# A delta-rule recurrence with a gated MLP: two batches in lockstep on four TensorE quadrants, every engine in a fixed order

## The chip, the core and the metric

The kernel runs on one core of one Trainium2 chip. The metric is the device time of one execution in microseconds (us). The core's engines are TensorE (PE; its weight loads are shown apart as PEld), VectorE (DVE), ScalarE (ACT), GpSimd (POOL) and SyncE (SP), which issues nearly all transfers. Each engine works through its own instructions in order; between engines there are semaphores.

## The reference

Four batches, eight heads, 768 positions, head size 48. Each head carries a 48x48 state through all positions; the heads' outputs, side by side (384), go through a gated MLP with a mix over positions.

```python
def _attn_ref(q, k, v, beta):
    k_n = k / (np.linalg.norm(k, axis=-1, keepdims=True) + 1e-06)
    for t in range(S):
        kt, vt, bt = (k_n[:, :, t], v[:, :, t], beta[:, :, t, None])
        y[:, :, t] = np.einsum('bhd,bhde->bhe', q[:, :, t], state)
        v_old = np.einsum('bhde,bhd->bhe', state, kt)
        state = state + bt[:, :, :, None] * np.einsum('bhd,bhe->bhde', kt, vt - v_old)

def _moe_ref(x, w_in, w_spatial, b_spatial, w_out):
    h = np.maximum(x @ w_in, 0.0)
    u, v = (h[..., :d_ff // 2], h[..., d_ff // 2:])
    v_n = (v - mean(v)) / np.sqrt(var(v) + 1e-06)
    v_s = np.einsum('ts,bsd->btd', w_spatial, v_n) + b_spatial[None, :, None]
    return (u * v_s) @ w_out
```

`w_in` and `w_out` arrive as float64 and are decoded on the chip by integer operations.

## The kernel before

**The recurrence.** The positions of a batch are cut into 12 chunks of 64; a step is one chunk of one batch, all 8 heads, so there are 48 steps. Heads lie in two halves of the partitions (h) and four units (u). Inside a chunk the recurrence is a triangular system: T is the inverse of a unit triangular matrix that is built from the products of the keys with themselves. Of each step:

- `products_mm` (line 360) multiplies keys with keys and with queries in one matmul 128 columns wide, and `products_out` masks and scales both halves on VectorE.
- For each group of 4 steps, `bounce` (L396) writes the triangular matrices to DRAM (tile `ad`), `load_la` (L502) reads them back turned, so that 128 lanes each hold half of a 32x32 block, and `lanes` (L538) inverts the blocks on VectorE by 30 rounds of a product (L550) and an addition (L557). The result goes to DRAM again (`wd`) and back (`ta`). There are 12 such groups. Group 0 takes a variant with 16x16 blocks (`lanes16`, L432).
- `step_t`, `step_e`, `step_f` (L583 to L610) widen the two 32x32 inverses to one of 64x64: a 32x32 transpose on VectorE and two rounds of matmuls with copies by ScalarE.
- `step_a` (L644) subtracts what the state holds for the keys from the scaled values, `step_b` (L662) multiplies by T and scales the result by -beta/norm² (L673), `step_c` (L680) adds to the state, and `step_d` (L696) forms the outputs in one matmul of 112 or 128 rows, for which `step_k` (L657) copies the masked products beside the queries.

`step_order` sets the order: two chains, batches 0 then 2 and batches 1 then 3, are interleaved from the sixth step on, so that the stages of one lie between those of the other. A matmul on f32 operands is two records on TensorE in the trace, on `float32r` operands one.

**The MLP.** Every tensor is held as a high and a low `float32r` part, and a product is three matmuls (high by high, high by low, low by high). Four chunks (256 positions) make one input: `convert` (L730) moves the last heads by six small DMAs and splits it; `mlp_v` (L762) and `mlp_u` (L820) form the two halves of the hidden layer, `post_v` normalizes; when a batch is complete `mlp_g` (L839) mixes over positions, `post_g` gates, `mlp_o` (L887) projects. `fill` (L924) feeds these matmuls in small portions between the stages of the recurrence.

**What sets the order.** `slot_a`, `slot_cd` and `slot_b` call the stages of a step with `pump`, `lane` and `fill` between them; the framework's scheduler orders the rest, and VectorE's order is written out by hand in the start-up phase alone. SyncE's queue carries the bounce, the loads of each step (`prefetch_*`, L619 to L633), the small moves of `convert`, the weights and the output.

Of the kernel before, what the change touches and what calls it, by code (L numbers as in the profile page):

```python
# [7 lines left out]
F32 = mybir.dt.float32  # L8
# [4 lines left out]
AX = mybir.AxisListType  # L13

NB, NH, SEQ, HD = 4, 8, 768, 48
CH = 64
NC_ = SEQ // CH
NST = NB * NC_
NU = NH // 2
G = 4  # L20
# [4 lines left out]
NG2 = NB * NT // 2  # L25
ND = DH // 128
KR = 112
EPS = 1e-6
R0 = 1.5
TD = 1  # L30
TP = 4
G16 = 1
C16 = 1
W16 = 16
X1 = 14
R1 = 1.7
CAP = 3.0
NL = 4
LD = 3
XD = 3  # L40
HP = 300
NW = 3
EJ = 6
PD = 2
M3 = 99
M4 = 12
CI = 1
CQ = 0
LS = 2
LP = 0  # L50
CAP0 = 4.0
PE0 = 18
PG0 = 99
PG1 = 99
VN = 1
VL = 1
DEC = 1
M5 = 10
DQ = 2
LAG = 6  # L60


def step_order():
    x = [(0, b, c) for b in (0, 2) for c in range(NC_)]
    y = [(1, b, c) for b in (1, 3) for c in range(NC_)]
    n = len(x) - LAG
    return x[:LAG] + [t for k in range(n) for t in (x[LAG + k], y[k])] + y[n:]


ORDER = step_order()  # L70
VB = 8
UB = 4
KQB=2
NPA=3
NPQ=2
# [3 lines left out]
def delta_rule_gated_mlp(  # L79
    ctx: ExitStack,  # L80
    tc: tile.TileContext,
    kq_t: bass.AP,
    kp_t: bass.AP,
    qb_t: bass.AP,
    qa_t: bass.AP,
    kv_nat: bass.AP,
    b_nat: bass.AP,
# [7 lines left out]
    PSUM = bass.MemoryType.PSUM  # L95
    const = ctx.enter_context(tc.tile_pool(name="const", bufs=1))
    grp = ctx.enter_context(tc.tile_pool(name="grp", bufs=2))
    live = ctx.enter_context(tc.tile_pool(name="live", bufs=3))
    work = ctx.enter_context(tc.tile_pool(name="work", bufs=2))
    moe = ctx.enter_context(tc.tile_pool(name="moe", bufs=2))  # L100
    dram = ctx.enter_context(tc.tile_pool(name="dram", bufs=2, space=bass.MemoryType.DRAM))
    pa = ctx.enter_context(tc.tile_pool(name="pa", bufs=NPA, space=PSUM))
    pq = ctx.enter_context(tc.tile_pool(name="pq", bufs=NPQ, space=PSUM))
    pm = ctx.enter_context(tc.tile_pool(name="pm", bufs=7 - NPA - NPQ, space=PSUM))
    pw = ctx.enter_context(tc.tile_pool(name="pw", bufs=1, space=PSUM))

    mpos = const.tile([128, CH], F32, name="mpos")
    nc.gpsimd.memset(mpos, 1.0)
    for h in range(2):
        nc.gpsimd.affine_select(  # L110
            out=mpos[h * 64 : h * 64 + 64],
            in_=mpos[h * 64 : h * 64 + 64],
            pattern=[[1, CH]],
            compare_op=ALU.is_gt,
            fill=0.0,
            base=0,
            channel_multiplier=-1,
        )

    bbc = const.tile([128, SEQ], F32, name="bbc")  # L120

    hm = const.tile([128, 1], F32, name="hm")
    nc.gpsimd.memset(hm, 1.0)
    for q in range(4):
        nc.gpsimd.memset(hm[q * 32 : q * 32 + 16], 0.0)

    mcs = [const.tile([128, NU, CH], F32, name="mc0")]
    sus = []
    for i in range(4):
        su = const.tile([128, 2 * NU * HD + 16], F32, name=f"su{i}")  # L130
        nc.gpsimd.memset(su, 0.0)
        sus.append(su)

    def su_view(t, h, u, rows, w=HD):
        o = (h * NU + u) * HD
        return t[rows, o : o + w]

    def su_all(t, h, rows):
        o = h * NU * HD
        return t[rows, o : o + NU * HD].rearrange("p (u e) -> p u e", e=HD)  # L140

    win_h = const.tile([128, NK, DFF], F32R, name="win_h")
    win_l = const.tile([128, NK, DFF], F32R, name="win_l")
    wsp_h = const.tile([128, NT, SEQ], F32R, name="wsp_h")
    wsp_l = const.tile([128, NT, SEQ], F32R, name="wsp_l")
# [1132 lines left out]
```

## Time and profile before

| | us |
|---|---|
| median of 3 runs | 654.91 |
| lowest, highest | 650.52, 655.48 |
| span of the profiled execution | 656.1 |

The page of a profile has the busy time of each engine and its share of the span, the span in 40 slices with the busy share in tenths, the clock that TensorE was granted, the chain of work that ended last, and the costliest groups of instructions with their mean duration and the idle time of the engine before them. Matmuls are pipelined and their ends are modelled, so they overlap in the records: the busy time of a group of matmuls is longer than the time that it takes. TensorE's pace has to be read from the starts in the timeline.

### The profile page before, as it was taken

To read this page: it belongs to the slowest core of one execution; us is meant where nothing else is said; L and a number is where in the kernel's file an instruction comes from. 1 tells how busy PE (TensorE), PEld (TensorE's weight loads), DVE (VectorE), ACT (ScalarE), POOL (GpSimd) and SP (SyncE) were. 2 spreads that over 40 slices of the span, in tenths; PEclk is the share of its full clock that TensorE was granted. 3 is DMA by queue.
4 is the path that set the end of the run, shared out by engine and by line. 5 is a ranking of instruction groups with operands and counts; after the bars stand their busy time and mean duration, and the time that the engine had idled before them with its cause. 6 is when DMAs were issued, how large, how long until landed. Compare 5 with 4: busy or idle time off the path is not lost.

```text
span 656.1 us, 19076 instructions
## 1 busy us (share of the span) xinstructions
PE 547.0 (83%) x7432; PEld 478.4 (73%) x7432; DVE 407.1 (62%) x1565; ACT 270.7 (41%) x732; POOL 201.0 (31%) x251
## 2 busy tenths in 40 slices
PE   5327657785578689799999898998998999999997
PEld 4316546664567568689888776888897789998997
DVE  3579978778878768485684868626727632223142
ACT  1124233563246256452524554624227674215421
POOL 4114544654343132224432323233213134310000
PEclk9999955787579679799999898898998999999999
DMA  8553576876654653634647465253254231101001
GB/s 241 128 132 97 149 173 170 229 170 167 180 114 119 163 117 104 119 109 113 127 131 163 113 139 130 86 117 94 78 124 89 66 66 48 52 15 41 1 25 49
DMA packets 144522, 74.63 MB, mean 114 GB/s; under 512 B 105136, under 2 KB 128432, under 8 KB 144432
## 3 DMA queue, kind: packets, MB, share of 16 engines
q1 hardware_dynamic: 144432, 73.41, 44.3%
q8 instruction: 59, 0.97, 0.6%
q14 instruction: 31, 0.25, 0.1%
HBM read 58.16 MB, written 14.02 MB: 110 GB/s over the span
## 4 chain that ended last, share of the span: by engine, by line
PE 53%; DMA 17%; DVE 14%; SPq 6%; issue 4%; ACT 4%; POOL 1%; DVEq 0%; ACTq 0%; POOLq 0%
PE pm L849 13%; PE pm L830 7%; PE pm L894 6%; PE pa L702 4%; DVE wstage L157 4%; PE pa L669 3%; PE pm L769 3%; PE pq L360 3%; PE pa L688 3%; PE pa L652 3%; DMA wstage<-in_w_out 2%; DMA wstage<-in_w_in 2%; PE pa L607 2%; PE pma L849 2%; DMA kqa<-in_qa_t 2%
## 5 line engine op out<-in xcount | busy, mean ns | idle before, releaser
L557 DVE TENSOR_TENSOR pw<-pw,prod 128x120 f32<-128x120 f32 (+4 forms) x300 | 75.8, 253 | 6.6
L849 PE MATMUL pm<-wsp_h,vl 128*128 128x256 f32 x252 | 73.1, 290 | 0.0
L849 PE MATMUL pm<-wsp_h,vh 128*128 128x256 f32 x252 | 72.4, 288 | 0.0
L849 PE MATMUL pm<-wsp_l,vh 128*128 128x256 f32 x252 | 71.5, 284 | 0.0
L360 PE MATMUL pq<-kq 128*64 128x128 f32 x640 | 57.6, 315 | 10.9 <-DVE wstage L157 4.4
L638 POOL TENSOR_TENSOR v<-v,cn 128x192 f32<-128x192 f32 x48 | 24.4, 509 | 111.9 <-DMA v<-in_kv_nat 95.6
L360 PEld LDWEIGHTS pq<-kq 128*64 128x64 f32 x640 | 42.9, 157 | 18.9 <-issue 13.4
L550 DVE TENSOR_TENSOR prod<-pw,la 128x30 f32<-128x30 f32 (+4 forms) x150 | 36.6, 244 | 24.2 <-ACT pw L529 18.6
L702 PE MATMUL pa<-kqa,su 128*64 128x64 f32 (+1 forms) x768 | 43.6, 248 | 8.4 <-DVE v L655 8.4
L673 DVE TENSOR_TENSOR su<-pa,cn 64x192 f32<-64x192 f32 x96 | 33.9, 353 | 26.6 <-PE pa L669 25.4
L652 PE MATMUL pa<-su,kqa 48*64 48x48 f32 x704 | 34.6, 238 | 18.6 <-DMA kqa<-in_qa_t 11.9
L669 PE MATMUL pa<-v,ta 64*64 64x48 f32 x768 | 41.5, 242 | 9.2 <-DVE v L655 5.5
L849 PEld LDWEIGHTS pm<-wsp_h,vl 128*128 128x128 f32 x252 | 47.7, 189 | 1.6 <-issue 0.9
L652 PEld LDWEIGHTS pa<-su,kqa 48*64 48x64 f32 x704 | 28.6, 149 | 27.7 <-issue 17.4
L849 PEld LDWEIGHTS pm<-wsp_h,vh 128*128 128x128 f32 x252 | 47.7, 189 | 1.1 <-issue 0.5
L849 PEld LDWEIGHTS pm<-wsp_l,vh 128*128 128x128 f32 x252 | 47.7, 189 | 0.4
L610 ACT COPY ta<-pa 32x128 f32<-32x128 f32 x96 | 24.4, 254 | 56.9 <-PE pa L607 56.0
L669 PEld LDWEIGHTS pa<-v,ta 64*64 64x64 f32 x768 | 33.1, 152 | 16.2 <-ACT win_h L205 5.9
L702 PEld LDWEIGHTS pa<-kqa,su 128*64 128x64 f32 (+1 forms) x768 | 33.9, 154 | 15.0 <-DVE v L655 9.4
L342 POOL TENSOR_TENSOR mc<-mpos,cn 128x256 f32<-128x256 f32 x44 | 27.0, 614 | 52.5 <-DVE ta L157 45.3
L655 DVE TENSOR_TENSOR v<-v,pa 128x192 f32<-128x192 f32 x44 | 15.3, 349 | 41.3 <-PE pa L652 40.9
L660 ACT COPY kqa<-ta 64x256 f32<-64x256 f32 x96 | 38.3, 399 | 3.0 <-PE pa L702 2.2
(151 smaller groups left out, 1343.7 us busy)
## 6 DMA issues: line engine op xcount, KB each, us to landing
kq<-in_kp_t SPq DMA_DIRECT2D x40, 384.0 KB, 3.5
ad<-ta SPq DMA_DIRECT2D x24, 256.0 KB, 3.9
kqa<-in_qb_t SPq DMA_DIRECT2D x48, 128.0 KB, 2.8
kqa<-in_qa_t SPq DMA_DIRECT2D x48, 96.0 KB, 2.6
v<-in_kv_nat SPq DMA_DIRECT2D x48, 96.0 KB, 2.4
knat<-in_kv_nat SPq DMA_DIRECT2D x48, 96.0 KB, 2.5
out<-ob SPq DMA_DIRECT2D x24, 192.0 KB, 1.9
kn<-in_kv_nat SPq DMA_DIRECT2D x20, 192.0 KB, 3.2
```

The costliest lines, as they stand in the source:

```text
L342: nc.gpsimd.tensor_tensor(out=mcs[s % len(mcs)], in0=mpos.unsqueeze(1).broadcast_to([128, NU, CH]), in1=cn_g[s // G][:, s % G, 1].unsqueez ...
L360: nc.tensor.matmul(p1[rows_t(h), u], kq[:, h, u, :], kq[:, h : 3 : 2 - h, u, :], start=True, stop=True,)
L550: (nc.gpsimd if PG0 <= g < PG1 else nc.vector).tensor_tensor(out=pr, in0=w[:, :n, j : j + 1].broadcast_to([128, n, m]), in1=(la[:, j, j + ...
L557: nc.vector.tensor_add(out=w[:, :n, j + 1 : 32], in0=w[:, :n, j + 1 : 32], in1=pr)
L652: nc.tensor.matmul(pr[rows_t(h), u], kqa[rows_d(h), 1, u, :], su_view(su, h, u, rows_d(h)), start=True, stop=True)
L660: nc.scalar.copy(out=kqa[rows_t(h), 2 - 2 * h], in_=aqk[rows_t(h)])
L669: mark["pb"] = nc.tensor.matmul(pu[rows_t(h), u], tt[rows_t(h), u, :], r[rows_t(h), u, :], start=True, stop=True)
L673: mark["db"] = nc.vector.tensor_tensor(out=su_all(su, h, rows_t(h)), in0=pu[rows_t(h)], in1=cn[rows_t(h), 1].unsqueeze(2).broadcast_to([64 ...
L702: nc.tensor.matmul(py[rows_t(h), u], su_view(su, h, u, kr, 64), kqa[kr, 2 - 2 * h, u, :], start=True, stop=True)
L830: nc.tensor.matmul(pu[:, k], w[:, kt, d0 : d0 + 128], a[:, kt], start=(n == 0), stop=(n == 3 * NK - 1))
L849: nc.tensor.matmul(p[:, k], v[i][:, d0 : d0 + 128], w[:, si, ts], start=(n == 0), stop=(n == 3 * NT - 1))
L894: nc.tensor.matmul(po[:, :DM], a[:, d, ts], w[:, d], start=(n == 0), stop=(n == 3 * ND - 1))
```

## The change

The kernel is written anew around a plan. The main parts:

- Batches 0 and 1 run in lockstep, then 2 and 3: a step is one chunk of two batches, 16 matrices, 24 steps, 6 groups of 4 steps (`NP`, `NG`).
- Each small matmul runs on one of four 64x64 quadrants of TensorE. `COMBOS` is the order of the quadrants; the two quadrants that write the same PSUM partitions write different banks.
- The recurrence is unscaled: the factor beta/norm² goes into the triangular matrix before it is inverted, and so T carries it. The scaled masks and the scaling of L673 are gone; the values are multiplied by the norm (`scale_v`).
- The lanes are turned by VectorE's 32x32 transposes of a whole group, without DRAM. A lane now inverts a whole 32x32 block: 31 rounds, up to 256 elements each.
- Products of keys with keys (`kk`), keys with queries (`kq`), queries with the state (`qs`) and the masked products with the new values (`pu`) are stages of their own; `qs` and `pu` accumulate in PSUM.
- Every instruction is an `Op` with engine, duration, priority and the names that it reads and writes. `Plan.run` plays them through a list scheduler with its own table of durations, and the kernel emits them in that order on all engines under `manual_schedule`.
- A step's keys, queries, values and keys by position are one load (`bun`), two buffers deep; keys come once more for `prep`.
- The MLP has the same matmuls. Input, high and low parts (`xh`, `xl`) are single, as is the gate's buffer until the last step gives its PSUM banks and the two `xt` buffers to the pools. Six `full` buffers hold the split v of one batch; the odd batch of a pair is split when the gate of the even one is done. The gate's product and low part are always GpSimd's.

The diff, cut to its core (the removed functions are those named above; the order is that of the new file):

```diff
-G = 4
+NP = 2 * NC_
+GP = 4
+NG = NP // GP
+NS = 8
+class Plan:
+    LAT = {"PE": 0.2, "DVE": 0.06, "ACT": 0.08, "POOL": 0.08, "SP": 0.0, "X": 0.0}
...
+    P.pool("pq", [0])
+    P.pool("pm", [6, 7])
+    P.pool("xs", [0, 1])
+    P.pool("x", [0])
+    P.pool("raw", range(NRAW))
+    P.pool("full", range(NFULL))
+    P.pool("u", range(NU))
+    P.pool("st", ["g0"])
+    P.pool("g", [])
...
+    COMBOS = ((0, 0), (1, 1), (0, 1), (1, 0))
...
+    def prep(g):
...
+            def kk(ke=ke, view=view):
+                for jp in range(4):
+                    for d, a in COMBOS:
+                        k = ks(ke, 0, d, a, jp % 2, jp // 2)
+                        mm(view[a * 64 : a * 64 + 64, d * 512 + jp * 64 : d * 512 + jp * 64 + 64], k, k)
...
+        P.add("DVE", 1.3, lambda: nc.vector.transpose(
+            out=v3(la, 32), in_=xg()[:, :, 0:32].rearrange("p b c -> p c b")), rd=xp("d0") + [("za", 0), ("za", 1)], wr=["la"] + xp("z1"), pr=base - 930)
...
+        P.add("DVE", 1.2, lambda: nc.vector.scalar_tensor_tensor(
+            out=la3, in0=la3, scalar=-1.0, in1=dv.unsqueeze(1).broadcast_to([128, 32, 32]), op0=ALU.mult, op1=ALU.mult),
+            rd=["dv"], wr=["la"], pr=p0)
...
+        for j in range(31):
+            n, m = j + 1, 31 - j
+            pt = pr_[:, : n * m].rearrange("p (a b) -> p a b", b=m)
+
+            def mul(j=j, n=n, m=m, pt=pt):
+                nc.vector.tensor_tensor(
+                    out=w3[:, :1, 1:32] if j == 0 else pt, in0=w3[:, :n, j : j + 1].broadcast_to([128, n, m]),
+                    in1=la3[:, j, j + 1 : 32].unsqueeze(1).broadcast_to([128, n, m]), op=ALU.mult)
+
+            def add(j=j, n=n, pt=pt):
+                nc.vector.tensor_add(out=w3[:, :n, j + 1 : 32], in0=w3[:, :n, j + 1 : 32], in1=pt)
...
+        P.add("DVE", 1.3, lambda: nc.vector.transpose(
+            out=xg()[:, :, 0:32].rearrange("p b c -> p c b"), in_=w3.rearrange("p i t -> p t i")),
+            rd=["wl"], wr=xp("d0") + xp("z1"), pr=p0 + 3)
...
+    def kqt(s):
...
+        P.add("PE", 0.62, kq, rd=[("bn", s % 2, "k"), ("bn", s % 2, "q")], wr=[("kq", s), ("pt", s % 2)], pr=300 + s, acq=[("pq", h)])
+        P.add("DVE", 0.69, lambda: nc.vector.tensor_tensor(
...
+            rd=[("kq", s), "mpos"], wr=[("pt", s % 2)], pr=300 + s, rel=[("pq", h)])
...
+    def step(s):
...
+            P.add("PE", 0.52, a_, rd=[bk("k"), "S"], wr=["pc"], pr=pr)
+            v2 = v3(b[:, V : V + 384], 192)
+            P.add("DVE", 0.55, lambda: nc.vector.tensor_tensor(out=v2, in0=v2, in1=v3(pc, 512)[:, :, 0:192], op=ALU.subtract),
+                  rd=["pc"], wr=[bk("v")], pr=pr)
...
+            P.add("PE", 0.62, qs, rd=[bk("q"), "S", "pc", "yev", ("pt", s % 2)] + [("x", sl, q) for q in ("d0", "o0", "z1", "d1")], wr=[("y", s)], pr=s + 0.5, acq=yacq)
...
+        P.add("PE", 0.52, b_, rd=[bk("v"), ("y", s)] + [("x", sl, q) for q in ("d0", "o0", "z1", "d1")], wr=["pc"], pr=pr)
+        P.add("ACT", 0.48, lambda: nc.scalar.copy(out=v3(w, 192), in_=v3(pc, 512)[:, :, 0:192]), rd=["pc"], wr=[("w", s % 2)], pr=pr)
+        if c < NC_ - 1:
...
+            P.add("PE", 0.52, c_, rd=[bk("n"), ("w", s % 2)], wr=["pc"], pr=pr)
...
+                P.add("DVE", 0.55, lambda: nc.vector.tensor_tensor(out=sv, in0=sv, in1=pv, op=ALU.add), rd=["pc"], wr=["S"], pr=pr)
...
+        P.add("PE", 0.62, pu, rd=[("w", s % 2), "yev", ("pt", s % 2)], wr=[("y", s)], pr=200 + s, acq=() if c else yacq)
...
+    def split_v(i):
+        f, r = Hold(), raw_h[i]
+        full_h[i] = f
+        kk, q = ("vr", i), 440 + i
+        P.add("ACT", 0.6, lambda: nc.scalar.copy(out=full_(f)[:, 0:DH], in_=raw_(r)), rd=[kk, ("gdone", i // NT - 1)], wr=[("vh", i)], pr=q, acq=[("full", f)])
...
+    prep(0)
+    weights()
+    load(0)
+    load(1)
+    prep(1)
+    for s in range(NP):
+        g = s // GP
+        widen(s)
+        scale_v(s)
+        kqt(s)
+        step(s)
+        if s + 2 < NP:
+            load(s + 2)
+        if s % 2:
+            mlp(s // 2)
+        if s % GP == GP - 1 and g + 2 < NG:
+            prep(g + 2)
+        if s % NC_ == NC_ - 1:
+            gate(2 * (s // NC_))
+            gate(2 * (s // NC_) + 1)
+    order = P.run()
+    with tc.manual_schedule():
+        for o in order:
+            if o.fn is not None:
+                o.fn()
```

The numbers after the engine's name in `P.add` are the plan's own durations in us; they set the order only.

1645 lines of the change are left out of this document (558 added, 1087 removed).

## The prediction

> **What bounds the kernel now.** I read the page's shares and slices first, then the chain that ended last, and then the timeline of TensorE for the true pace of each kind of matmul.
>
> ```profile
> PE 547.0 (83%) x7432; PEld 478.4 (73%) x7432; DVE 407.1 (62%) x1565; ACT 270.7 (41%) x732; POOL 201.0 (31%) x251
> PE   5327657785578689799999898998998999999997
> PEclk9999955787579679799999898898998999999999
> PE 53%; DMA 17%; DVE 14%; SPq 6%; issue 4%; ACT 4%; POOL 1%; DVEq 0%; ACTq 0%; POOLq 0%
> ```
>
> TensorE (PE) is the busiest engine and half of the chain, but its first 250 us (15 slices) are half empty and its granted clock is mostly 0.5 to 0.8 there: transfers (17%), VectorE (14%) and SyncE's queue (6%) set the pace of the recurrence, and the MLP's matmuls are left for the end. The page's busy shares are no pace, since matmuls overlap. The pace is the distance from one group's start to the next group's start:
>
> ```profile
> 451.91 1.09 PE L360 MATMUL pq<-kq 128*64 128x128 f32 x16
> 452.94 0.67 PE L652 MATMUL pa<-su,kqa 48*64 48x48 f32 x16
> 453.53 0.44 PE L607 MATMUL pa<-ta,pi 32*32 32x32 f32 x16
> 453.90 0.56 PE L688 MATMUL pa<-su,knat 64*48 64x48 f32 x16
> 454.39 0.44 PE L894 MATMUL pm<-wout_h,gh 128*128 128x384 f32 x1
> ...
> 457.26 0.69 PE L702 MATMUL pa<-kqa,su 112*64 112x64 f32 x16
> 457.87 0.67 PE L669 MATMUL pa<-v,ta 64*64 64x48 f32 x16
> 458.47 0.44 PE L595 MATMUL pa<-tn,ta 32*32 32x32 f32 x16
> 458.84 0.38 PE L849 MATMUL pm<-wsp_h,vl 128*128 128x256 f32 x1
> ...
> 607.17 1.40 PE pm L769 x6
> 613.13 1.40 PE pm L830 x12
> ...
> 635.38 4.26 PE pma L849 x36
> 639.64 2.09 PE pm L894 x12
> ```
>
> Small stages: 1.03 (L360), 0.59, 0.37, 0.49, 0.61 (L702), 0.60, 0.37: 4.06 us for one step of 8 heads, 48 steps, 195 us. MLP: 24 groups of 9 matmuls of L769 at 1.40/6, 432 of L830 at 1.40/12, 864 of L849 at 4.26/36, 288 of L894 at 2.09/12: 50 + 50 + 102 + 50 = 253 us (the last four rows are of the chain). Together 448 us of matmul time in a span of 656.1 us: about 208 us of TensorE is waiting or slow clock. The sum below is of this execution; its span is 0.2% over the median of 654.91, and I leave that out.
>
> **The change part by part.**
>
> *Matmuls.* The MLP's 253 us stay: same shapes and counts, both types as before. A small stage now issues 16 products (32 records, as every f32 product is two) on four 64x64 tiles instead of 8 on two. What speaks for four at once:
>
> ```profile
> 48.51 0.41 PE L490 MATMUL pa<-ta,prod 32*16 32x16 f32 x32 [0.59 <-ACT prod L484]
> 131.57 1.09 PE L669 MATMUL pa<-v,ta 64*64 64x48 f32 x16
> 132.59 0.59 PE L595 MATMUL pa<-tn,ta 32*32 32x32 f32 x16
> ```
>
> L490 puts 32 records on four 32-row tiles in 0.41 us, L595 16 records on two tiles in 0.44 (458.47): four tiles do run side by side. There each tile has its own rows and columns. In the new order two of the four share rows; L702 has two column halves on the same rows and takes 0.61, like L669 (0.60) with rows of its own. So I take L702's 0.61 for a stage of 64 columns with twice the products, 0.49 (L688) for 48. The upper end is two tiles at a time: L360 against L702, 64 more columns for 8 beats, is 0.42 us, so 1.03 per stage. I take the low end, because both kinds of sharing have a row. The two 32-wide stages keep two tiles and double their records: between 0.37 and 0.74, I take 0.65 (0.37 holds a fixed part). A pair of batches: 0.61 x 6 (kk, kq, a, qs, b, pu) + 0.49 (c) + 2 x 0.65 = 5.45 us, 24 steps: 131 us. TensorE falls from 448 to 384 us. That is the floor.
>
> [...]
>
> *Lanes.* The bounce through DRAM goes (ad, la, wd and ta transfers, 3 to 4 us each way and four in a row, off SyncE's queue as well), and so does L660's copy. VectorE turns a whole group of 4 pair steps (128 lanes x 32) by one 1024-element transpose each way and eliminates all 32 columns at once.
>
> ```profile
> 22.73 0.18 DVE L444 TENSOR_TENSOR prod<-la 128x14 f32<-128x14 f32 x1
> 22.94 0.17 DVE L451 TENSOR_TENSOR la<-la,prod 128x14 f32<-128x14 f32 x1
> ...
> 48.13 0.28 DVE L550 TENSOR_TENSOR prod<-w,la 128x120 f32<-128x120 f32 x1
> 48.44 0.28 DVE L557 TENSOR_TENSOR w<-w,prod 128x120 f32<-128x120 f32 x1
> L557 DVE TENSOR_TENSOR pw<-pw,prod 128x120 f32<-128x120 f32 (+4 forms) x300 | 75.8, 253 | 6.6
> L468 DVE STREAM_TRANSPOSE la<-ta 128x256 f32<-128x256 f32 x4 | 1.6, 430 | 1.2 <-DMA kqa<-in_qa_t 1.2
> L865 DVE TENSOR_TENSOR gt<-pm,bbc 128x512 f32<-128x512 f32 x21 | 14.4, 687 | 22.5 <-PE pm L849 22.3
> L655 DVE TENSOR_TENSOR v<-v,pa 128x192 f32<-128x192 f32 x44 | 15.3, 349 | 41.3 <-PE pa L652 40.9
> ```
>
> One after another, 14 elements cost 0.21 and 120 cost 0.31 us; L655 to L865 add 1.05 ns per element. So an operation is about 0.195 us + 1.05 ns per element. A group has 61 operations with 10,881 elements in all (twice the sum of (j+1)(31-j), less 31): 11.9 + 11.4 = 23.3 us. Two transposes (four times L468 would be 1.7, its slope gives less): 1.2 each. Scaling 1024 elements 1.2, twelve small operations at 0.2, a hop over ScalarE for the root 0.5: 30 us per group, 6 groups instead of 12. A pair step adds a transpose 0.43, the mask over 512 elements 0.69, two operations over 384 (between 0.35 and 0.69) 0.55 each: 2.2 us. A norm of two MLP tiles is 8 small operations, 1.6.
>
> *Decode of the float64 weights.* Half as many instructions, twice as wide.
>
> ```profile
> L157 DVE TENSOR_SCALAR wstage<-wstage 128x256 uint32<-128x256 uint32 (+1 forms) x80 | 26.9, 354 | 12.0 <-DMA wstage<-in_w_in 6.5 <-DMA wstage<-in_w_out 3.9 <-issue 1.3
> L157 DVE SCALAR_TENSOR_TENSOR wstage<-wstage 128x256 uint32<-128x256 uint32 (+3 forms) x40 | 16.9, 429 | 0.2
> ```
>
> A job of 512 columns has 4 + 2 of them: between 2.3 us (fixed cost alone) and 4.5 (all by element); 3.4, in the middle, as no row is nearer to an end. Six jobs for w_in.
>
> *Transfers.* A step's k, q, v and k-by-time come in one bundle of 896 KB in place of five transfers, two buffers deep (k once more, 256 KB, for the preparation).
>
> ```profile
> kq<-in_kp_t SPq DMA_DIRECT2D x40, 384.0 KB, 3.5
> kq<-in_kq_t SPq DMA_DIRECT2D x8, 224.0 KB, 5.4
> xs<-xs SPq DMA_DIRECT2D x72, 16.0 KB, 1.8
> ```
>
> Between 3.5 and 8.2 us (in proportion to 384 KB); I take 6.5. The bundle for step s+2 waits until step s has been read, so it costs about 1 us every other step in a run of steps; on SyncE's in-order queue the six xs copies stand behind their step and may hold a bundle back, another 0.5. When TensorE is full the cover is its backlog.
>
> *The step's chain.* a, subtract, b, copy, c, add. A stage takes 0.72 us until its reader starts (L669 at 457.87, its reader in VectorE at 458.59, quoted next), and 0.42 more at half clock (L669 needs 1.02 at 131.57, 0.60 at 457.87).
>
> ```profile
> 458.59 0.72 DVE L673 TENSOR_TENSOR su<-pa,cn 64x192 f32<-64x192 f32 x2 [0.31 <-PE pa L669]
> L903 ACT COPY ob<-pm 128x384 f32<-128x384 f32 x19 | 9.1, 478 | 14.0 <-PE pm L894 8.5 <-DMA out<-ob 1.8 <-POOL vl L815 1.5
> ```
>
> 3 x 0.9 + 2 x 0.55 + 0.48 + three hops back of 0.15 + half an MLP piece (0.35) three times: 5.3 us. The one pair of banks for products (pq) is new: kq, then the outputs' qs, b, copy, pu and copy hold it in turn, about 5.0 us per step, just inside the chain.
>
> *When TensorE gets its backlog.* Until the gates can start, VectorE is the bound. First transpose at 14 us: first products at 5.5 as now, the third k tile needs the first one's buffer, 3 to 5 us, then copy and shift 3. One w_in job fits before. Then three preparations 3 x 30 = 90, five jobs 17, eight steps 8 x 2.2 = 18, norms of four MLP pairs 6: 145 us. Then group 2's four steps, 4 x 5.3 + 3 for the shift back and the bundle: 169. The last two MLP inputs share one xh/xl buffer: from step 9's end (158), copies, cast and split 9, v and u 8.4, cast and split 3, v 4.2, norm and split of v 8.5: 191. VectorE's order is fixed, so part of the half clock's 0.42 us per stage (12 steps x 2 stages, 10 us at most) stays: 5. The gates start at about 196 us.
>
> By then TensorE has done 12 steps (65), the next group's kk (2.5) and 5.5 MLP pairs (46): 114. Left: 384 - 114 = 270 us. How full it runs is read from 500 to 650 us now (rows of L849, L830, L769, L894):
>
> ```profile
> 500.00:650.00 150.00, 55.32 (x432) 52.60 (x432) 1.00 0.15 41
> 500.00:650.00 150.00, 23.73 (x180) 22.14 (x180) 1.00 0.15 41
> 500.00:650.00 150.00, 18.42 (x72) 12.99 (x72) 1.00 0.15 41
> 500.00:650.00 150.00, 29.96 (x156) 26.54 (x156) 1.00 0.15 41
> ```
>
> By their paces 51 + 21 + 17 + 27 = 116 us, and seven steps without kq of 3.03 are 21 to 23: 139 of 150, 93%. So 270 / 0.93 = 290. Between gates 2 and 3 six v tiles are split on GpSimd, in series, since they reuse the first batch's buffers:
>
> ```profile
> L882 POOL TENSOR_TENSOR gl<-gt,gh 128x512 fp32r<-128x512 f32 x16 | 20.5, 1279 | 27.7 <-ACT gh L880 27.7
> ```
>
> 6 x 1.28 + 2.6 for the gate before, less 4.2 of output matmuls: 6 us. The last gate's add, product, cast and split and the output's copy and transfer: 6 more. 196 + 290 + 12 = 498 us. The second half of the recurrence hides under the backlog: VectorE needs 6 x 30 + 24 x 2.2 + 12 x 1.6 + 24 x 0.69 (gates) + 31 (decode) = 300 us in all, so its last group ends near 305 even if nothing else covers it. GpSimd keeps both of a half gate's operations to the end (today's last gates use VectorE): 2 x 1.28 us under 4.26 of matmuls. The scaled masks and L673's scaling go, GpSimd and ScalarE stay under half busy: I cost that at nothing, with TensorE's backlog as cover.
>
> **The rivals.**
> A, TensorE is fuller: the fixed order hides the cold start and leaves 3% idle. The gates start at 175 (decode at 2.3 us, no stalls, shorter waits for the J5 input), 270 / 0.97 = 278, +6: 459. For it: 50.00 of 50 us busy late in the run now; against: one gate buffer and one xh/xl until the recurrence ends.
> B, the tiles that share rows run in turn: seven stages x 0.42 = 2.9 per step, 12 steps / 0.93 = 38, and 5 in the chain before: 541.
> C, the order, fixed for a full clock, breaks at half clock: six hand-offs per step late by 0.42 on engines that cannot pass by, 24 steps: 60, less the 5 counted: 553. For it: PEclk 5 to 7 in the first half; against: VectorE and TensorE both have other work queued.
> D, the other side: VectorE's lanes become the bound of the whole. Recurrence end = 12 + 6 x (61 d + 7) + 95 of other VectorE work (steps, decode, norms), then 100 for J11 and two gates. It reaches 655 when d is 1.1 us, against 0.38 worked out here and L557's 0.25 measured. Only an unseen price of the strided reads would do that.
> E, no change: the second half waits as the first does now. The DMA share of the chain is gone, so little speaks for it.
>
> [...]
>
> **How the numbers follow.** Forecast (470 to 525) 0.45; A (445 to 470, a little below) 0.22; B (525 to 560) 0.13; C (525 to 600) 0.13; D 0.04; E 0.03. Range 445 to 565: below lies 0.05, above half of C, D and E. One per cent is about what can be told from no change. Faster 0.93, same 0.03, slower 0.04. Predicted: 498 us.
>
> **What would show it.** Right: a 32-record stage on four tiles starts its successor 0.6 us later; a lane group near 30 us of VectorE; the gate matmuls first seen at 185 to 205 us, after which PE's slices read 9 and the clock 1; no ad or wd transfers. Wrong: stages of 1.0 us at full clock (B), gaps on TensorE that wait for VectorE late in the run (C, D), a gate start before 175 (A).

## The result, and the profile after

| | before | after |
|---|---|---|
| median, us | 655.19 (4 runs beside those of the change) | 579.7 (4 runs) |
| lowest to highest | 650.52 to 658.55 | 579.29 to 583.8 |
| span of the profiled execution | 656.1 | 577.3 |

The ratio is 0.8874 (95% interval 0.882 to 0.8928): 11% faster. The forecast was 498 us in a range of 445 to 565, so the direction was right and the time is 82 us longer than forecast. Two executions of all runs below (one of e1b, one of e17) were in a slower state of the chip and are left out of the medians.

From the page of the kernel after: the busy time of the engines, TensorE's slices and granted clock, and the chain that ended last.

```profile
PE 450.4 (78%) x8520; PEld 402.9 (70%) x8520; DVE 321.4 (56%) x719; ACT 208.6 (36%) x452; POOL 206.8 (36%) x175
PE   2100697965986879677988796999999977899997
PEclk9999999977588885869899897999999978899999
PE 48%; DVE 29%; issue 8%; ACT 6%; DMA 5%; POOL 2%; SPq 1%; POOLq 0%; ACTq 0%; DVEq 0%
q8 instruction: 66, 1.08, 0.8%
```

The transfers have nearly left the chain (17% to 5%), as the change meant. In their place stand VectorE (14% to 29%) and "issue" (4% to 8%), time in which an engine waits for nothing that the profile shows. The last line is the queue that brings instructions: 66 packets of 16 KB.

The timeline of TensorE in the kernel after, first at full clock, then in the first group of steps, then where the first gate matmul (`wsp_h,vf`) starts:

```profile
316.63 0.68 PE L335 MATMUL ps<-s,bn 48*64 48x48 f32 x32
317.24 0.39 PE L335 MATMUL ps<-wsp_h,vf 128*128 128x256 f32 x1
...
318.15 0.67 PE L335 MATMUL ps<-bn,s 48*48 48x64 f32 x32
318.63 0.63 PE L335 MATMUL ps<-bn,xt 64*64 64x48 f32 x32
319.20 0.69 PE L335 MATMUL ps<-tn,xt 32*32 32x32 f32 x32
...
66.94 1.13 PE L335 MATMUL ps<-ke 48*64 48x64 f32 x32 [0.15 <-DMA ke<-in_k_t]
67.82 1.08 PE L335 MATMUL ps<-bn,xt 64*64 64x48 f32 x32
68.83 1.06 PE L335 MATMUL ps<-tn,xt 32*32 32x32 f32 x32
...
275.75 0.39 PE L335 MATMUL ps<-wsp_h,vf 128*128 128x256 f32 x1
```

From start to start, a stage of 32 records on four quadrants takes 0.61, 0.48 and 0.57 us at 316 us: the pace that was forecast. At 67 us such stages take 0.9 to 1.0 (`bn,xt` 1.01 instead of 0.57): half clock, although the page gives 9 for that slice. In this trace the clock's record begins at 105 us only (in e5 and e6 it is 0.50 from 62 to 94 us). The gates start at 275.8 us, not at 196.

Where the time goes, by three rows of the windows view of the kernel after (busy times of PE, PEld, DVE, ACT and POOL with their instructions, the clock, the transfers):

```profile
16.00:182.80 166.80, 101.05 (x2602) 87.51 (x2596) 144.37 (x313) 60.73 (x127) 58.22 (x45) 0.90 0.30 98
59.00:276.00 217.00, 171.16 (x4390) 146.87 (x4391) 183.63 (x416) 95.66 (x220) 77.22 (x68) 0.83 0.29 95
276.00:577.00 301.00, 273.03 (x3940) 250.54 (x3939) 95.31 (x219) 98.99 (x216) 112.05 (x90) 0.95 0.14 45
```

The first ends where the last transpose of the third lane group starts; that one ends at 185.0. From VectorE's timeline of the same kernel:

```profile
182.80 2.21 DVE L418 STREAM_TRANSPOSE xt<-wl 128x1024 f32<-128x1024 f32 x1
```

From 59 to 276 us neither TensorE (171 of 217 us) nor VectorE (184) is full, and together they are busy far longer than the stretch.

VectorE's groups of the kernel after, with their mean in ns:

```profile
L406 DVE TENSOR_TENSOR ps<-wl,la 128x60 f32<-128x60 f32 (+9 forms) x180 | 88.1, 489 | 5.3
L411 DVE TENSOR_TENSOR wl<-wl,ps 128x60 f32<-128x60 f32 (+9 forms) x180 | 61.5, 342 | 5.4
L418 DVE STREAM_TRANSPOSE xt<-wl 128x1024 f32<-128x1024 f32 x6 | 13.1, 2187 | 0.2
L379 DVE STREAM_TRANSPOSE la<-xt 128x1024 f32<-128x1024 f32 x6 | 11.9, 1985 | 2.9 <-POOL xt L374 2.9
```

The forecast took 0.38 us for an operation of either kind. The additions (L411) cost 0.34, the products (L406) 0.49, and a transpose 2.0 to 2.2 us instead of 1.2. Which products cost more is seen in the timeline of GpSimd and VectorE:

```profile
33.53 3.42 POOL L268 TENSOR_TENSOR wsp_l<-g,wsp_h 128x1536 fp32r<-128x1536 f32 x1 [2.53 <-ACT wsp_h L267]
33.62 3.55 DVE L406 TENSOR_TENSOR ps<-wl,la 128x192 f32<-128x192 f32 x1
```

This product, whose two inputs both lie in SBUF, takes 3.55 us and ends 0.2 us after GpSimd's subtraction (37.17 and 36.95); one of as many elements takes 0.37 us at 54.01, with no GpSimd instruction beside it. Over the whole trace, the 131 products that overlap no GpSimd instruction average 354 ns, and the 49 that do 852. The additions, with one input in PSUM, show no difference (341 and 345 ns).

### The profile page after: what moved, and what is told of

It is laid out like the page before. It is cut to its first block, busy times and chain, and to the rows that moved or that the text cites. A ratio compares the mean times of both kernels' runs of the same rounds, so it can differ in the third digit from the quotient of the medians.

```text
span 577.3 us, 19065 instructions
## 1 busy us (share of the span) xinstructions
PE 450.4 (78%) x8520; PEld 402.9 (70%) x8520; DVE 321.4 (56%) x719; ACT 208.6 (36%) x452; POOL 206.8 (36%) x175
## 4 chain that ended last, share of the span: by engine, by line
PE 48%; DVE 29%; issue 8%; ACT 6%; DMA 5%; POOL 2%; SPq 1%; POOLq 0%; ACTq 0%; DVEq 0%
PE ps L335 48%; DVE ps L406 10%; DVE wl L411 7%; DVE xt L418 2%; DMA g<-in_w_sp 2%; DMA bn<-in_bun 2%; ACT vr L631 1%; SPq L243 1%; DVE pt L480 1%; ACT junk L616 1%; DVE st L625 1%; DVE s L548 1%; POOL xl L584 1%; DVE la L395 1%; DVE tn L435 1%
## 5 line engine op out<-in xcount | busy, mean ns | idle before, releaser
L335 PE MATMUL ps<-wsp_h,vf 128*128 128x256 f32 x576 | 122.2, 298 | 1.8 <-ACT vf L639 0.9
L335 PEld LDWEIGHTS ps<-wsp_h,vf 128*128 128x128 f32 x576 | 97.4, 198 | 4.3 <-ACT vf L639 1.1
L406 DVE TENSOR_TENSOR ps<-wl,la 128x60 f32<-128x60 f32 (+9 forms) x180 | 88.1, 489 | 5.3
L335 PE MATMUL ps<-wsp_l,vf 128*128 128x256 f32 x288 | 83.6, 290 | 0.0
L411 DVE TENSOR_TENSOR wl<-wl,ps 128x60 f32<-128x60 f32 (+9 forms) x180 | 61.5, 342 | 5.4
L640 POOL TENSOR_TENSOR vf<-vr,vf 128x512 fp32r<-128x512 f32 x24 | 30.8, 1292 | 86.4 <-ACT vf L639 86.3
L701 POOL TENSOR_TENSOR gt<-gt,ut 128x512 f32<-128x512 f32 x24 | 31.2, 1300 | 72.6 <-DVE gt L698 72.6
L335 PEld LDWEIGHTS ps<-wsp_l,vf 128*128 128x128 f32 x288 | 57.1, 198 | 0.0
L335 PE MATMUL ps<-win_h,xh 128*128 128x512 f32 x72 | 29.0, 506 | 10.2 <-ACT xh L583 10.2
L335 PE MATMUL ps<-wout_h,g 128*128 128x384 f32 x128 | 35.7, 345 | 0.7 <-POOL g L704 0.7
```

Of the source, the lines that this page charges most:

```text
L335: nc.tensor.matmul(o, l, r, start=start, stop=stop)
L406: nc.vector.tensor_tensor(out=w3[:, :1, 1:32] if j == 0 else pt, in0=w3[:, :n, j : j + 1].broadcast_to([128, n, m]), in1=la3[:, j, j + 1 : ...
L411: nc.vector.tensor_add(out=w3[:, :n, j + 1 : 32], in0=w3[:, :n, j + 1 : 32], in1=pt)
L640: P.add("POOL", pool_t(512), lambda: nc.gpsimd.tensor_sub(out=full_(f)[:, DH : 2 * DH], in0=raw_(r), in1=full_(f)[:, 0:DH]), rd=[kk, ("vh" ...
L701: P.add("POOL", pool_t(512), lambda: nc.gpsimd.tensor_mul(out=gt_[t.unit], in0=gt_[t.unit], in1=u_(uh)[:, half * 512 : half * 512 + 512]), ...
```

## The experiments

Two theories came first: V, VectorE's unforeseen prices (products beside GpSimd, transposes, decode) hold the first half back; O, the planned order does, since its table of durations is wrong on this chip. All times below are medians in us; the change is 579.7.

**e1_replan.** The durations in the plan's table are set to those of the trace; only the order changes.

```diff
-        P.add("DVE", 1.3, lambda: nc.vector.transpose(out=v3(la, 32), ...
+        P.add("DVE", 2.0, lambda: nc.vector.transpose(out=v3(la, 32), ...
-                P.add("DVE", dve_t(n * m), mul, ...
+                P.add("DVE", dve_t(n * m) * 1.35 + 0.03, mul, ...
```

> The changed kernel with the plan's table of durations set to those of its own trace (the turned transposes 2.0 and 2.2 us instead of 1.3, small VectorE operations 0.2 to 0.4 instead of 0.1, lane products 1.35 times, decode operations 1.2 times, w_in's load 5.6 us); no instruction changes, only the order. Theory O (the loss of the first half is the order: made for other durations, so that engines wait for each other): the gates' first matmul comes at 235 us or earlier instead of 276, the time is 545 us or less. Theory V (VectorE's prices bound the first half, whatever the order): the gates start at 265 or later, the time stays at 565 us or more.

577.2 (576.84 to 578.45), though the gates start at 254.5, between what the two theories expected. An earlier gate start alone is worth next to nothing.

**e2_wpsum.** The lanes' result `wl` moves to PSUM banks 4 and 5 and the product to SBUF, so no lane operation has two SBUF inputs; the outputs of `widen` move to free columns.

```diff
-    pc, pq, pe, pr_ = ps[:, 0:1024], ps[:, 1024:2048], ps[:, 2048:2560], ps[:, 2560:3072]
+    pc, pq, wl = ps[:, 0:1024], ps[:, 1024:2048], ps[:, 2048:3072]
+    pe, pf = ps[:, 192:448], ps[:, 704:960]
```

> The lanes' matrix W stands in PSUM (two banks) and the product in SBUF, so that no lane operation reads two SBUF tensors; the two small stages of the widening move to free columns of the state's banks; W is cleared by ScalarE instead of GpSimd. The plan's durations are as in the changed kernel. [...]

572.2 (568.45 to 575.33), ratio 0.8708 (0.8657 to 0.876), gates at 263.5. The product's group in this kernel:

```profile
L408 DVE TENSOR_TENSOR prod<-ps,la 128x60 f32<-128x60 f32 (+9 forms) x180 | 62.1, 345 | 5.4
```

489 to 345 ns, 26 us of VectorE's work; by theory V the time had to fall by about as much, and it fell by 7. That a product into PSUM might be slow in itself is ruled out by the trace of the change: beside no GpSimd instruction it takes 354 ns there as well. So the price goes with two SBUF inputs beside GpSimd's work; by what means the one holds up the other, no run shows.

**e3_both.** e1 and e2 together.

> Both edits: W in PSUM and the plan's durations set to the measured ones (lane products at their price without waits). If V and O each hold a part and add up: 530 us or less, gates from 225 us. If V alone: as e2, within 8 us. If O alone: as e1, within 8 us.

570.5 (570.0 to 572.85), gates at 259. Neither V nor O explains 80 us.

**e4_more_gpsimd.** Two small GpSimd additions beside each lane product, read by nothing.

```diff
+                for k in range(2):
+                    P.add("POOL", 0.02, lambda: nc.gpsimd.tensor_add(out=scr, in0=la[:, 0:48], in1=la[:, 64:112]), rd=["la", "wl"], pr=9000)
```

> The changed kernel with two small additions on GpSimd beside each lane round (360 of about 0.2 us, two SBUF inputs, nobody uses the result). [...]

583.1, and the products' mean went from 489 to 474 ns. If any GpSimd instruction beside a product made it longer, the mean had to rise: a miss. Additions this short (0.33 us each, which makes up all of GpSimd's rise from 207 to 325 us busy) did not lengthen the products. Why they did not, the run does not show.

The "issue" share of the chain is the next question. The timeline of TensorE in the kernel after, in the third group of steps, at full clock up to 211.2 us:

```profile
207.48 0.52 PE L335 MATMUL ps<-pt,w 64*48 64x64 f32 x24
209.15 0.33 PE L335 MATMUL ps<-pt,w 64*48 64x64 f32 x8 [1.16 <-issue]
209.41 0.69 PE L335 MATMUL ps<-tn,xt 32*32 32x32 f32 x32
210.03 0.68 PE L335 MATMUL ps<-s,bn 48*64 48x48 f32 x32
210.53 0.66 PE L335 MATMUL ps<-bn 48*64 48x64 f32 x32
211.12 0.82 PE L335 MATMUL ps<-xt,pi 32*32 32x32 f32 x23
213.91 0.47 PE L335 MATMUL ps<-xt,pi 32*32 32x32 f32 x9 [1.97 <-issue]
```

Stages break in the middle, where the profile shows no wait for a semaphore ("issue", 1.16 and 1.97 us). From one break to the next are 8 + 32 + 32 + 32 + 23 = 127 records (one is missing from the trace), each with a weight load: 256 instructions. That is about one 16-KB packet of the instruction queue, as 17,040 matmuls and weight loads over 66 packets are 258 each (in the kernel before, 14,864 over 59 are 252). Theory F: in a burst of small matmuls TensorE runs out of instructions. Theory C: the half clock, however it comes, is what makes the steps slow. Theory B: the 896-KB loads stand in the way.

**e5_bench.** Forty stages of the four-quadrant kind, on the constant mask, where TensorE waits for the first lanes.

```diff
+            for k in range(4):
+                for d, a in COMBOS:
+                    mm(ps[a * 64 : a * 64 + 64, d * 512 + 448 : d * 512 + 512], mpos[d * 64 : d * 64 + 64], mpos[d * 64 : d * 64 + 64])
```

> Forty stages of 32 records on four 64x64 tiles, on the constant mask, are added back to back where TensorE waits for the first lane group (20 to 62 us); nothing reads them. They are 2,560 instructions, ten blocks of 256. Theory F (TensorE runs out of instructions in a burst of small records: a 16-KB block of the instruction queue holds 256 of them, and its packets follow each other at 3.5 us or more in the trace after): the forty take at least 10 x 3.5 = 35 us, with pauses one block apart, whatever the clock. Theory C (half clock alone): 1.05 us a stage for the first few, then 0.61 each, some 26 us in all and no pauses. With C the first steps after them also run at 0.6 a stage instead of 1.06, so that the second lane group begins some 10 us before 94; with F it begins where it did, within 4 us.

579.5. The timeline of TensorE in e5:

```profile
18.64 6.53 PE L335 MATMUL ps<-mpos 64*64 64x64 f32 x285
25.59 2.09 PE L335 MATMUL ps<-mpos 64*64 64x64 f32 x128 [0.42 <-issue]
29.32 2.09 PE L335 MATMUL ps<-mpos 64*64 64x64 f32 x128 [1.64 <-issue]
...
37.05 2.09 PE L335 MATMUL ps<-mpos 64*64 64x64 f32 x128 [1.64 <-issue]
41.87 2.09 PE L335 MATMUL ps<-mpos 64*64 64x64 f32 x128 [2.73 <-issue]
...
50.15 3.26 PE L335 MATMUL ps<-mpos 64*64 64x64 f32 x128 [2.46 <-issue]
53.61 1.95 PE L335 MATMUL ps<-mpos 64*64 64x64 f32 x99 [0.19 <-issue]
```

Theory F fits what e5 shows. After the first 285 records, each 128 records (256 instructions) run in 2.1 us and then TensorE stands; the next block comes 3.73 to 4.82 us after the last. (Only the block at 50.15, at half clock from 50.7 on, fills its own time: the next comes after 3.46.) In the same trace a packet of the instruction queue lands 1.34 to 1.60 us before each of these blocks starts: at 24.18, 27.89 and 35.65 for those at 25.59, 29.32 and 37.05. (In the change such packets start 3.3 us apart at the least, not 3.5.) The forty stages took 37 us (18.6 to 55.6) instead of some 20. So in e5, where stages follow each other without rest, a stage of 64 instructions cost about 0.9 us (3.46 / 4 to 3.73 / 4) at the least, whatever its own 0.5 or 0.6.

**e6_warm and e7_warm_both.** The idle stretches of TensorE's planned order are filled with products of the mask by itself, in the change (e6) and in e3 (e7).

```diff
+            for _ in range(n):
+                mm(ps[0:64, 448:512], mpos, mpos)
```

> In the changed kernel TensorE's idle stretches of the planned order are filled, up to the last step, with 367 multiplications of the mask by itself (64 columns, nothing reads them), 180 of them in the wait for the first lane group. Theory C (the slow first half comes from the half clock: 82 us of TensorE's work lie in half-clock stretches): the granted clock from 62 to 276 us rises above 0.95, gates begin at 235 to 250 instead of 275.8, and the whole is 545 to 560. Rival S (TensorE's speed is covered by VectorE, which is busy 184 of the 217 us, and by instruction supply): the clock rises, and gates begin within 10 us of 275.8; the time is 570 to 590, the fillings' own hindrance among it.

> The same fillings on the version with the lane products kept in PSUM and measured durations in the plan (570.5 us, gates at 259). There VectorE has some 25 us less to do in this stretch, so theory C should show more: gates at 215 to 235 and 530 to 548 us. Rival S: gates at 250 to 265 and 560 to 580 us.

591.2 and 588.5: slower than without. A filling took 0.12 us instead of the planned 0.2, so those of e6's first wait ended at 41 us, and the clock from 62 to 94 us was 0.50 all the same. The later fillings (322 records in e6) lie between the steps' stages; that they made the run slower is likely but not shown. Nothing on theory C follows.

**e8_small_bundles.** The loads of steps 2 to 23 are cut to 64 of 1792 columns.

```diff
-        ld(bnd[s % 2], bun[s], ...
+        ld(*((bnd[s % 2], bun[s]) if s < 2 else (bnd[s % 2][:, 0:64], bun[s][:, 0:64])), ...
```

> The loads of the bundles of steps 2 to 23 are cut to their first 64 of 1792 columns, so these steps compute with old values. Theory B (the 896-KB loads hold up the fetch of TensorE's instructions, and the records themselves): pauses of 2 to 3 us between blocks of 256 instructions fall to about 1, the chain's share of issue falls from 8% to about 4%, and the time is 555 to 565. Rival: the loads lie beside other work, and the time is 574 to 580 with the same pauses.

578.6 (577.38 to 579.76). The waits view (total, times, longest), of the kernel after:

```profile
PEld ps L335 <- issue: 19.9, 28, 2.9
```

and of e8:

```profile
PEld ps L335 <- issue: 10.3, 19, 1.8
```

Theory B is right about the pauses (with the loads cut, half of their total is gone, and the longest is 1.8 us instead of 2.9) and wrong about the time: it did not move.

**e9_warm_start and e12_warm_start_both.** 350 fillings in the first wait alone, so that they last until the steps begin; the same with 300 in e3.

> The fillings of e6 lay too short (0.12 us each at full clock: they ended at 40 us, and the steps from 62 on were at 0.50 again). Here 350 of them fill the wait for the first lane group alone, nothing is added anywhere else. Theory C: the first group's steps (62 to 100 us) run at full clock, stages of 32 records take 0.6 us instead of 1.06, and the second lane group begins at 82 to 88 us instead of 94.2; the whole gains 4 to 12 us. Theory F (instruction supply, shown by e5: 256 instructions per 3.7 us at best): the clock is full but pauses of 1 to 2 us appear at every 256 instructions, and the second lane group begins at 90 to 95; the whole within 3 us of 579.7.

> 300 fillings in the wait for the first lane group, on the version with the lane products in PSUM and measured durations (570.5 us, second lane group at 98, gates at 259). Theory C: second lane group at 86 to 92, and the whole 558 to 567, the best so far. Theory F: second lane group at 94 to 99 and 568 to 573.

578.5 and 573.2: no gain. The second lane group of e9 began at 94.8 as before (94.2), that of e12 at 101.2. The timeline of TensorE in e9:

```profile
69.80 0.66 PE L335 MATMUL ps<-pt,w 64*48 64x64 f32 x30
73.94 0.34 PE L335 MATMUL ps<-pt,w 64*48 64x64 f32 x1 [3.47 <-issue]
```

and its windows:

```profile
60.00:70.00 10.00, 8.23 (x366) 7.51 (x367) 8.58 (x13) 6.13 (x12) 6.85 (x6) 1.00 0.41 124
70.00:74.00 4.00, 0.53 (x34) 0.38 (x27) 3.96 (x6) 0.88 (x2) 3.69 (x4) 0.99 0.96 344
74.00:101.00 27.00, 22.53 (x739) 20.57 (x739) 21.71 (x37) 10.35 (x21) 13.10 (x10) 0.50 0.36 124
```

The steps began at full clock (1.00). Then TensorE stood 3.5 us at the end of a block while the transfer engines were 96% busy; the clock fell to 0.50 and stayed there for 27 us, though TensorE's records cover 22.5 of them. In e12 the steps began at 56.6, also at full clock, and no long pause came before the fall. From the timeline of TensorE and the windows of e12:

```profile
60.91 1.33 PE L337 MATMUL ps<-ke 48*64 48x64 f32 x32 [0.41 <-DMA ke<-in_k_t]
...
50.00:61.00 11.00, 10.51 (x309) 10.02 (x307) 7.39 (x11) 4.90 (x9) 4.38 (x4) 1.00 0.15 36
61.00:66.00 5.00, 4.41 (x146) 3.88 (x148) 3.95 (x7) 3.03 (x8) 2.79 (x2) 0.53 0.48 135
```

The clock fell at 61.3, after 4.7 us of small stages whose longest wait was 0.41 us.

**e13_warm_small.** e9 and e8 together.

> The 350 fillings of e9 together with the cut loads of e8 (steps 2 to 23 compute with old values). In e9 the clock was full at 60 us and fell at 70.5, after TensorE had stood 3.7 us at a boundary of 256 instructions with the transfer engines 97% busy. If pause and load cause the fall (theory F-C): no pause above 2 us there, the clock stays above 0.9 from 62 to 95, a stage takes 0.6, the second lane group begins at 82 to 89 and gates at 258 to 270. If the small stages themselves lose the clock whatever the loads: 0.5 to 0.6 again from 75 on, the second lane group at 92 to 96.

570.4 (567.51 to 573.33). The windows of e13:

```profile
60.00:66.00 6.00, 4.44 (x176) 4.04 (x178) 5.37 (x10) 3.90 (x7) 5.00 (x5) 1.00 0.23 68
66.00:97.00 31.00, 26.72 (x927) 24.56 (x921) 28.90 (x42) 13.82 (x28) 18.93 (x15) 0.51 0.22 67
```

With the long pause gone the clock fell all the same, at 66 us, and the second lane group began at 91.7. So the long pause is not needed: the steps, with waits of 0.7 and 0.9 us for ScalarE (to 63.5 and 65.7) here and almost none in e12, came to half clock too (0.51 and 0.53). Whether the pause alone would have cost it in e9 is not shown. What the first group would take at full clock was not reached by any run.

**e10, e11, e14.** Half of the products of six stages of each step left out (`range(4)` becomes `(0, 3)`); all products of the lanes' rounds left out (the additions add zeros); both. The order is the same in all.

> Half of the matrix products of each step's stages are left out (8 of 16 in each of the six), the order and all waits unchanged: some 57 us less of TensorE's work at full clock and 4,200 fewer instructions. Theory P (TensorE's own rate, half clock and instruction supply, is what holds the first half back): gates begin at 215 to 240 us instead of 275.8, and the whole is 510 to 535. Theory V (VectorE is the bound there): gates at 262 to 275 and the whole 560 to 575. Theory L (the two take turns, each waiting for the other): between, gates at 240 to 262 and 535 to 560.

> The 180 products of the lanes' rounds are left out (the additions add zeros): 88 us less of VectorE's work, the order and all other waits unchanged. Theory V: gates begin at 205 to 225 us and the whole is 500 to 525. Theory P: gates at 258 to 275 and 560 to 578. Theory L: gates at 225 to 258 and 525 to 560.

> Half of the steps' products (e10: 27 us gained, gates at 260) and all products of the lanes' rounds (e11: 41 us gained, gates at 244) left out together. Theory L (TensorE and VectorE take turns on one chain, so their shares add): 68 us or more gained against 579.7, 500 to 515, gates at 222 to 232. If each is hidden by the other in part, taking both away gains more than the sum: below 500. If a third thing bounds (loads, ScalarE, GpSimd): 520 to 536, gates at 236 to 244.

The first line of the page of e10:

```profile
PE 415.5 (76%) x6312; PEld 366.9 (67%) x6312; DVE 320.7 (58%) x719; ACT 207.2 (38%) x452; POOL 207.8 (38%) x175
```

and of e11:

```profile
PE 445.6 (83%) x8520; PEld 400.8 (75%) x8520; DVE 242.6 (45%) x540; ACT 208.5 (39%) x452; POOL 206.6 (39%) x175
```

| | left out | time | gain | gates start | last step's output | end of span |
|---|---|---|---|---|---|---|
| after | | 579.7 | | 275.8 | 456.6 | 577.3 |
| e10 | 2,208 records, 42 us at 0.61 per 32 | 553.0 | 27 | 260.3 | 429.0 | 549.7 |
| e11 | 79 us of VectorE | 538.9 | 41 | 243.7 | 417.0 | 534.9 |
| e14 | both | 507.3 | 72 | 233.8 | 388.3 | 506.1 |
| e1 | nothing | 577.2 | 3 | 254.5 | 464.3 | 576.7 |

(The 57 us in the expectation of e10 were an error: it is 42.) Theory L holds. Each engine's part is worth something alone, about half to two thirds of its work, and together they are worth 72, their sum of 68 and a little more. Engines that cover each other would give little alone and much together. The gates of e14 started 2 us later than expected. What TensorE's part holds (half clock, supply of instructions, the stages themselves) these runs do not take apart.

The table shows one thing more: from the last step's output to the end are 112 to 121 us in every row, with and without changes to the rest. In the kernel after, 38 matmuls of `mlp_v`, 108 of `mlp_u`, 432 of gates and 144 of `mlp_o` start there, 98 us by the paces of the prediction (8.9 + 12.6 + 51 + 25). The end is the recurrence's end plus this tail; the gates' start by itself is not what sets it. The orders planned with measured durations show that best: their gates start at 254.5 (e1), 259.1 (e3), 273.6 (e16) and 274.3 (e15), and their tails are 112, 111, 112 and 113 us all the same, 8 to 10 shorter than the change's.

**e15, e16, e1b, e17: is there a better order?** All with measured durations in the plan; e15 on e2's layout with TensorE 1.3 times as long before 270 us and eight `raw` buffers, e16 without the eighth buffer, e1b on the change's own layout, e17 like e15 but with the small stages alone made longer.

```diff
-            free[e] = t + o.dur
+            d = o.dur * (1.3 if e == "PE" and t < 270 else 1.0)
+            free[e] = t + d
```

> The version with products in PSUM, planned with measured durations and TensorE's stages 1.3 times as long before 270 us, and eight buffers for unsplit tiles instead of seven. If the order's mismatch with the slow first half costs something: 555 to 566. If not: 567 to 575, no better than the 570.5 of the version it starts from.

> As e15 with seven buffers for unsplit tiles, as in the change. If the order planned for a slow TensorE makes e15's gain: 558 to 564. If the eighth buffer makes it: 567 to 573.

> The change with measured durations and TensorE's stages 1.3 times as long before 270 us in the plan, nothing else: order alone, lane products in SBUF. If order and the place of the products gain apart from each other (7 us for the place in e2, some 10 for the slow plan): 565 to 572. If the slow plan only helps where VectorE has less to do: 574 to 580.

> As e15, but the plan makes only the small stages 1.6 times as long (0.62 to 0.99, what the trace shows at half clock), up to 300 us, and the MLP's matmuls keep their time. If a plan nearer to the trace gives a better order: 545 to 558. If the order beyond e15 makes no difference: 558 to 565.

| | time | ratio to before, 95% |
|---|---|---|
| e3 | 570.5 | 0.8694 (0.866 to 0.8728) |
| e16 | 564.1 | 0.8607 (0.8569 to 0.8645) |
| e15 | 560.3 | 0.8555 (0.8503 to 0.8608) |
| e1b | 573.2 | 0.8732 (0.868 to 0.8784) |
| e17 | 597.0 | 0.9078 (0.902 to 0.9137) |

Planning with the slow first half gains 6 us (e3 to e16); the eighth buffer's 4 are within the intervals. So is e1b's gain of 4 over e1, and its time lies between its two theories: what the slow plan is worth without the products' new place stays open. e15 beats both kernels, some 3.5% below the change; its gates start at 274.3, as late as the change's, and its last step's output comes at 446.1 instead of 456.6. e17, whose plan seemed nearer to the trace, is worse than the change: a miss. A durations table nearer to the trace in one place does not make the planned order better.

## Why the prediction was wrong, step by step

*Right.* The pace of the stages: 0.48 to 0.61 us for 32 records on four quadrants at full clock, where 0.49 and 0.61 were taken. Rival B falls here, and with it its 1.03 us for a stage: the four quadrants, each of which shares its rows with another, ran side by side. First transposes at 14 us (16.0). The transfers nearly left the path; a bundle took 4.9 us in the median (6.5 taken).

*Mis-sized terms.* Lane products 489 ns instead of 382 (additions 342), transposes 2.0 and 2.2 us instead of 1.2: VectorE was busy 321 us in all instead of 300. e2 shows what the products' price is worth: 7 us. And the terms of the step's chain, as they are written, add up to 5.8 us and not to 5.3, 2 us for four steps.

*The step that failed* is "Until the gates can start, VectorE is the bound", and with it "The second half of the recurrence hides under the backlog". The sum laid VectorE's lanes without a gap, and TensorE's steps and the MLP beside them. The milestones show it:

| | predicted | measured |
|---|---|---|
| third preparation ends | 145 | 185.0 |
| group 2's steps end (its last output) | 169 | 227.7 |
| gates start | 196 | 275.8 |
| lanes end | near 305 | 349.4 |

From 16.0 to 185.0 VectorE did 147 us of work (the first of the three windows and the transpose behind it) where 131 were counted, and stood idle for 22: 2 late at the start, 16 by price and 22 by waiting make the first 40. Then four steps took 43 us instead of 24. Half of the 19 more came before the first step's output at 202.6: GpSimd's shift back took until 191.0, 6 us where 3 were counted for shift and bundle, and between the two rounds of the widening TensorE worked through 39 MLP matmuls, from 186.6 to 195.3, as the order had them. The timeline of VectorE in the kernel after has two state updates and what they waited for:

```profile
202.13 0.55 DVE L548 TENSOR_TENSOR s<-s,ps 112x384 f32<-112x384 f32 x1
...
207.79 0.56 DVE L548 TENSOR_TENSOR s<-s,ps 112x384 f32<-112x384 f32 x1 [0.45 <-PE ps L335]
...
217.88 0.55 DVE L548 TENSOR_TENSOR s<-s,ps 112x384 f32<-112x384 f32 x1 [2.10 <-PE ps L335]
```

5.7 and 10.1 us per step, against 5.3; between the last two stand the pauses before 209.2 and 213.9 that were shown above, and VectorE's fixed order makes the lanes behind the update wait as well. The last 21 of the 80 lie between group 2's end and the gates. There the timeline of TensorE has this:

```profile
241.64 1.01 PE L335 MATMUL ps<-win_h,xh 128*128 128x512 f32 x2 [0.55 <-ACT xh L583]
249.21 1.07 PE L335 MATMUL ps<-tn,xt 32*32 32x32 f32 x32 [6.56 <-DVE tn L435]
250.20 0.80 PE L335 MATMUL ps<-win_h,xh 128*128 128x512 f32 x1
```

TensorE stands 6.6 us for the fourth lane group, with the third matmul of the same MLP product queued behind the wait. A pause of 2.8 us before 275.2 and half clock from 241.9 to 255.6 are part of the rest; how the 21 divide is not shown. All this is rival C's mechanism, hand-offs late on engines that cannot pass by, with a chance of 0.13; its sum put the clock as the only cause, and it was held against it that both engines have other work queued. They do, but the fixed order keeps them from reaching it: e10, e11 and e14 show that what one engine loses, the other waits for.

*After the gates' start.* By then 129 us of matmuls were done and not 114, and by the measured stages 248 were left instead of 270; at 93% and with the 12 us for split and end that would be 279, and it took 301.5 (82%). The terms join: 80 later, 23 less to do, 23 emptier; 498 + 80 - 23 + 23 is the span's 577 within 1 us, and the median lies 2 above it. But e1, with gates 21 us earlier and the same end, shows that this milestone was the wrong one to sum from: the recurrence, planned to be hidden from 305 on, gave its last output at 456.6, and the tail of 121 us came after. Nor did VectorE hold it to the end, as its lanes were done at 349.4. ScalarE's timeline of the kernel after has the cast of the eighth MLP input:

```profile
373.28 0.83 ACT L583 CAST xh<-xs 128x768 fp32r<-128x768 f32 x1
```

That input was complete at 289.0, but it waited 84 us for the one `xh`, whose earlier input had its last matmuls at 368.5, among the gates of the first two batches; the next step's output came at 380.0, 57 us after the one before. So the second half did not hide under the backlog, it stood in line behind it. Which buffer is worth how much no run shows (e15's eighth `raw` gained no more than the noise). Rival D had that form (the recurrence's end plus 100 us), with its price per lane operation as the condition; the recurrence became late without that price.

*Not foreseen at all.* The supply of instructions. The change raises TensorE's instructions only from 14,864 to 17,040, but it packs the small ones into bursts. What this cost in time stays open: with the pauses halved (e8) the time did not move.

## What to carry to other kernels

Where two engines hand each other a chain in a fixed order, do not take the larger of their busy times: leave out a part of each, and of both, and see whether the gains add. For a burst of small matmuls count instructions as well as columns: in e5 a block of 256 took 3.46 to 4.82 us once the first blocks were used up. And sum from the work that ends last (here the recurrence and its tail), not from the milestone that is easiest to see.

## What the runs showed of the hardware

- In e5's dense burst TensorE stood, after the first 285 records, at every 256 instructions: 128 records in 2.1 us, the next block 3.46 to 4.82 us after the last, 1.34 to 1.60 us behind the landing of an instruction packet. With the 896-KB loads the longest such pause was 2.9 us (kernel after) and 3.5 us (e9, the transfer engines 96% busy); with small loads it was 1.8 us (e8).
- The clock fell without a long pause in e12: at 61.3 us, after 4.7 us of small stages whose longest wait was 0.41 us (1.00 before 61 us, 0.53 from 61 to 66). In e9 it stayed at 0.50 over 27 us in which TensorE's records covered 22.5.
- A product of VectorE with both inputs in SBUF lasted 3.55 us beside a GpSimd subtraction of 3.42 us that had started 0.1 us before; such products averaged 852 ns beside GpSimd instructions and 354 ns otherwise, and 345 ns with one input in PSUM (e2).
- A 128x1024 float32 transpose of VectorE with strided blocks took 1.9 to 2.2 us (kernel after).
- The record of the granted clock began late in the kernel after: none before 105 us, where stages of 0.9 to 1.0 us instead of 0.48 to 0.61 point to the half clock that e5 and e6 recorded there (0.50 from 62 to 94 us).
